# First batch's k and v loaded by halves of the heads, rms_g spread over the lanes by TensorE, the fifth tokens of q loaded behind the weights, and one turn of q issued behind the x turn

## The chip, the cores and the metric

The kernel runs on one core of one Trainium2 chip. The core has five engines that each work through their own instructions in order: TensorE (PE in the profile, with its weight loads as PEld), VectorE (DVE), ScalarE (ACT), GpSimd (POOL) and SyncE (SP), and 16 DMA engines that serve the queues of SP, ACT and POOL. Engines wait for each other by semaphores. The metric is the device time of one execution in microseconds; the time before is the median of three runs.

## The reference

The program is a linear attention with cosine weights, followed by a feed-forward block with an RMS norm and SwiGLU. With 8 batches, 8 heads, 576 tokens a batch and a head size of 64:

```python
r = np.maximum(x, 0.0); phi = np.concatenate([r * c, r * s], axis=-1)   # c, s: cos, sin of pi/2 * pos/S
kv = np.einsum('bhsf,bhsd->bhfd', k_p, v);  z = np.sum(k_p, axis=2)
num = np.einsum('bhsf,bhfd->bhsd', q_p, kv)
den = np.einsum('bhsf,bhf->bhs', q_p, z)[..., None] + 1e-06
x = (num / den).transpose(0, 2, 1, 3).reshape(B * S, H * D)             # 4608 x 512
xn = x / np.sqrt(np.mean(x * x, axis=-1, keepdims=True) + 1e-06) * rms_g
g = xn @ w_gate;  val = xn @ w_val                                      # 512 x 1536
out = (g / (1 + np.exp(-g)) * val) @ w_out                              # 1536 x 512
```

Inputs and output are float32.

## The kernel before

**Tiling.** A batch of 576 tokens is held in 128 lanes with four or five tokens a lane (`J = 4`, `NC5 = 5`); token slot `t` of all lanes is a tile of 128 tokens. Slots 0 to 3 of a batch make one block of 512 tokens; the fifth slots of two batches share a tile, and the four such tiles make a ninth block. The raw q, k and v lie in two buffers each (`qbuf`, `kbuf`, `vbuf`), so that batch `b` reuses the buffer of batch `b - 2`.

**A batch's attention.** `k_feat` makes the features of k: per slot two instructions, relu(k) times cosine and relu(k) times sine, on DVE or ACT (L246, L244). `v_cast` makes v bf16 (L258, L256). `kv_mm` (L291) multiplies them, 40 matmuls of 65 columns, and `kv_evict` copies the product to `kvm`: for batch 0 one half of the heads on ACT (L305) and the other on DVE (L307). `q_feat` makes the features of q, `q_turn` transposes them by a DMA of SP's queue (L316), or `q_turn_pe` does it on PE (L327) with `q_evict` after it (L336, L338). `num_mm` (L351) gives numerator and denominator, `divide` the quotient x (L377 to L389), `sumsq` the sum of squares on ACT (L400) and then its power of -1/2 on POOL (`rs`, L405), and `norm` multiplies x by `rs` and by `gb`, the gains rms_g in every lane (L410). The normed tile is transposed to `xnT` by `x_turn` (a DMA of SP's queue, L418) or `x_turn_pe` (L428) with `x_evict` (L435, L437).

**The feed-forward.** Nine blocks of twelve steps. A step makes 512 columns of gate and value products (L460 in pieces, L447 whole; tiles `gps`, `vps`), the silu on ACT (L685), the product on DVE (L695), and from block 2 on also the output products of the block before (L492). Block 0's output products are made in `lead()`, between blocks 0 and 1, with batch 1's attention in between.

**The order.** It is written out by hand. `at(g, w, f, ...)` puts work into place `w` of step `g` (12 steps to a block, counted through); the places run in the order sp, act0, dve0, mid, act1, act2, dve1, pe. `x_turn`s asked for under "sp" are issued right after dve0 of that step, work under "pe" after the step's matmuls. Each engine and each DMA queue works in this order; an instruction that waits holds up those behind it on its engine.

**The start.** SP issues the loads of batch 0: k, slots 0 and 1 of q, v, the gains broadcast to 128 lanes (`gb`, L138), slots 2 to 4 of q. Each load is two DMAs, one for the even and one for the odd lanes (L115). PE runs 44 matmuls on constants (`warm_up`), then the transposes of q. POOL makes constants, then `pool_after` (L238) copies one element of the first features of q, so that the weights, whose DMAs POOL issues next (L226, L232), come after them. From the ninth of POOL's DMAs on, each waits, by the built program, for the landing of the one eight before it. Batch 0's loads are all on SP's queue; from batch 1 to the k and v of batch 3 they are on POOL's, and later ones on SP's again.

Of the kernel before, what the change touches and what calls it, by code (L numbers as in the profile page):

```python
# [17 lines left out]
def kernel(  # L18
# [28 lines left out]
    def K(i):  # L47
        tc.keep_in_program_order(i)
        return i
# [27 lines left out]
    def gv_tile(shape, dtype, name):  # L77
        u = gv_out.pop(0)
        t = ps_gv.tile(shape, dtype, name=name, tag=f"gv{u}")
        gv_in[id(t)] = (u, t)  # L80
        return t

    def gv_read(t):

        if id(t) in gv_in:
            gv_out.append(gv_in.pop(id(t))[0])
# [20 lines left out]

    def load(t, src, b, odd_five=False, cuts=(0, NC5)):  # L110
        for lo, hi in zip(cuts[:-1], cuts[1:]):
            for par, t0, jn in lanes(odd_five):
                z = min(hi, jn)
                eng = nc.gpsimd if 0 < b < 3 or b == 3 and src is not q else nc.sync
                K(eng.dma_start(  # L115
                    out=t[par:P:2, :, lo * D : z * D],
                    in_=src[b, :, :, :].rearrange("h (i j) d -> i h (j d)", j=NT)[
                        :, :, (t0 + lo) * D : (t0 + z) * D
                    ],
                ))  # L120

    def load_v(b, cuts=(0, NC5)):
        load(vraw[b], v, b, False, cuts)

    def load_k(b):
        load(kraw[b], k, b)

    def load_q(b, cuts=(0, NC5)):
        load(qraw[b], q, b, b % 2 == 1, cuts)

    clear_fifth(kbuf[0], nc.vector)
    clear_fifth(qbuf[0], nc.vector)
    clear_fifth(vbuf[0], nc.vector)
    gb = consts.tile([P, DM], FP32, name="gb")
    load_k(0)
    load_q(0, (0, 2))
    load_v(0)
    K(nc.sync.dma_start(  # L138
        out=gb[:, :], in_=moe_rms_g.rearrange("(o d) -> o d", o=1).to_broadcast([P, DM])
    ))  # L140
    load_q(0, (2, NC5))


    iota_i = consts.tile([P, 1], mybir.dt.int32, name="iota_i")
# [41 lines left out]
    def table(c, u, j):  # L186
        n = u * J + j if j < J else 2 * J
        return trig[:, c, n : n + 1]
# [11 lines left out]
    vx = [consts.tile([P, H, E], BF16, name=f"vx{j}") for j in range(NC5)]  # L200
    kvm = [consts.tile([P, H, E], BF16, name=f"kvm{u}") for u in range(NK)]

    NX = 3
    xbuf = [consts.tile([P, DM + 1], FP32, name=f"x{u}") for u in range(NX)]
    for u in range(NX):
        nc.gpsimd.memset(xbuf[u][:, DM : DM + 1], math.sqrt(1e-6 * DM))
    warm = consts.tile([P, 2 * P], BF16, name="warm")
# [1 line left out]
    nc.vector.memset(warm[:, :], 1.0)  # L209
    for j in range(NC5):  # L210
        nc.gpsimd.memset(vx[j][:, :, D:E], 1.0)
    for t in (kbuf[1], qbuf[1], vbuf[1]):
        clear_fifth(t, nc.gpsimd)

# [9 lines left out]
    def load_gv(c):  # L224
        for (w, src) in ((wg, moe_w_gate), (wv, moe_w_val)):
            K(nc.gpsimd.dma_start(  # L226
                out=w[:, :, c * GC : (c + 1) * GC],
                in_=src[:, c * GC : (c + 1) * GC].rearrange("(t p) n -> p t n", p=P),
            ))
# [11 lines left out]
    def feat(dst, src, scale, act):  # L241

        if act:
            K(nc.scalar.activation(out=dst, in_=src, func=AF.Relu, scale=scale))  # L244
        else:
            K(nc.vector.tensor_scalar(  # L246
                out=dst, in0=src, scalar1=scale, scalar2=0.0, op0=ALU.mult, op1=ALU.max,
            ))

    def k_feat(b, j, c, act=False):  # L250
        feat(kp[j][:, :, c, :], kraw[b][:, :, j * D : (j + 1) * D], table(c, 0, j), act)

    def v_cast(b, j, act=False):
        src, dst = vraw[b][:, :, j * D : (j + 1) * D], vx[j][:, :, 0:D]
        if act:
            K(nc.scalar.copy(out=dst, in_=src))  # L256
        else:
            K(nc.vector.tensor_copy(out=dst, in_=src))  # L258
# [3 lines left out]
    def q_feat(b, t, c, act=False):  # L262
        if (b, t) not in qps:
            pool, tag = (qpp, "qp") if t < J else (qp5p, "qp5")
            qps[b, t] = pool.tile([P, H, 2, D], BF16, name=tag, tag=tag)
        feat(
            qps[b, t][:, :, c, :], qraw[b][:, :, t * D : (t + 1) * D], table(c, b % 2, t), act
        )

    def att_tile():  # L270

        return ring(ps_att, 2, [P, 2, TB], FP32, "att")

    def att_heads(a):
        return a[:, :, 0 : Z * E].rearrange("p z (s w) -> p z s w", w=E)

    def kv_banks(b):

        t = kvp[b]
        return t if b == 0 else [t[:, z, :] for z in range(2)]  # L280

    def kv_mm(b, j, first, last):
        if first:
            kvp[b] = (
                [gv_tile([P, TB], FP32, "kv0") for _ in range(2)]
                if b == 0 else att_tile()
            )
        banks = kv_banks(b)
        for h in range(H):

            K(nc.tensor.matmul(  # L291
                banks[h // Z][:, (h % Z) * E : (h % Z) * E + D + 1],
                lhsT=kp[j][:, h, :, :].rearrange("p c d -> p (c d)"),
                rhs=vx[j][:, h, 0 : D + 1],
                start=(first and h % Z == 0),
                stop=(last and h % Z == Z - 1),
            ))

    def kv_evict(b):
        dst = kvm[b % NK][:, :, :].rearrange("p (z s) w -> p z s w", z=2)  # L300
        if b == 0:
            for z, t in enumerate(kvp.pop(b)):
                src = t[:, 0 : Z * E].rearrange("p (s w) -> p s w", w=E)[:, :, 0 : D + 1]
                if z == 0:
                    K(nc.scalar.copy(out=dst[:, z, :, 0 : D + 1], in_=src))  # L305
                else:
                    K(nc.vector.tensor_copy(out=dst[:, z, :, 0 : D + 1], in_=src))  # L307
                gv_read(t)
        else:
            K(nc.scalar.copy(  # L310
                out=dst[:, :, :, 0 : D + 1], in_=att_heads(kvp.pop(b))[:, :, :, 0 : D + 1]
            ))

    def q_turn(b, t):
        tt = rqtp.tile([P, H, P], BF16, name="rqT", tag="rqT")
# [191 lines left out]
    def at(g, w, f, *a):  # L507
        plan[g, w].append(lambda: f(*a))
# [48 lines left out]
    at(3, "pe", x_turn_pe, (0, 3))  # L557
    at(4, "dve0", x_evict, (0, 3), 0, 3, True)
    for c in range(2):
        at(2 + c, "act2", q_feat, 0, J, c, True)  # L560


    at(0, "pe", load_wo, 2)
    at(0, "pe", load_k, 1)
    for f, *a in ((load_q, 1, (0, 2)), (load_v, 1), (load_q, 1, (2, NC5))):
        at(2, "pe", f, *a)
    for f in (load_k, load_q, load_v):
        at(3, "pe", f, 2)

    def pe_tile_at(g, key, xblk, col, gx, first="act1"):  # L570

# [29 lines left out]
        at(18, "act2" if j > 2 else "dve1", v_cast, 2, j, j > 2)  # L601
    kv_at(18, 2)
    pe_tile_at(19, (2, 0), 2, 0, 22, "act0")
    for t, g in enumerate((13, 19, 20, 21, 23)):
        q2_at(g, 2, t)
    pe_tile_at(22, (2, 1), 2, 1, 24)
    for t in (2, 3):
        tile_at(22 + t, (2, t), 2, t)


    at(15, "pe", load_q, 3)
    for j in range(NC5):
        for c in range(2):
            at(22 + j, "act2" if c else "dve1", k_feat, 3, j, c, c == 1)
# [152 lines left out]
            ))  # L767

    warm_up(44)
    for j in range(NC5):  # L770
        for c in range(2):
            if (j, c) in ((2, 1), (NC5 - 1, 1)):
                q_feat(0, 0, int(j > 2), act=(j > 2))
            k_feat(0, j, c, act=(j > 2))
    for c in range(2):
        q_feat(0, 1, c, act=(c == 1))
    pool_after(qps[0, 0][0:1, 0, 0, 0:1])
    for c in range(NG):
        load_gv(c)
    for c in range(2):  # L780
        load_wo(c)
    q_turn_pe(0, 0)
    q_evict(0, 0, dve=True)
    q_turn_pe(0, 1)
    q_evict(0, 1)
    warm_up(6)
    for j in range(NC5):
        v_cast(0, j, act=(j % 2 == 1))
    for j in (0, 1, 2, 4, 3):
        kv_mm(0, j, j == 0, j == 3)  # L790
    kv_evict(0)
    num_mm((0, 0))
    num_mm((0, 1))
    for c in range(2):
# [73 lines left out]
```

## Time and profile before

| | us |
|---|---|
| median of 3 runs (lowest to highest) | 332.92 (332.68 to 333.15) |
| the profiled execution's own time | 333.1 |
| its span, first to last instruction | 331.0 |
| busy: PE, DVE, ACT, POOL | 316.5, 189.5, 167.8, 42.7 |
| PE busy in the first 20 us | 13.50 |
| PE busy from 60 to 80 us | 18.25 |
| first gate product (L460) starts | 19.72 |

The profile lists, for each group of instructions, when they start, how long they take, and in square brackets how long the engine was idle before them and what ended the wait. A DMA's "us to landing" counts from the start of its issue until its data has arrived. About 2.1 us of the profiled time lie outside the span.

### The profile page before, as it was taken

The numbers are of one execution on the slowest core, as the hardware profiler recorded it, in microseconds if no ns is written. First come the engines' busy times: TensorE is split into PE (matmuls) and PEld (weight loads), VectorE is DVE, ScalarE is ACT, GpSimd is POOL, SyncE is SP. The second block draws the span as 40 slices with busy tenths as digits, with TensorE's granted clock in tenths as the row PEclk, the third lists the DMA queues.
The fourth block names the chain that finished last, engine by engine and source line by source line (L and its number), as shares of the span: only waits on it lengthen the run. The fifth ranks groups of instructions, "written<-read, shape, count | busy, mean of one in ns | idle before, by whom it ended". The sixth has DMA issues, their size and how long they took to land.

```text
span 331.0 us, 7153 instructions
## 1 busy us (share of the span) xinstructions
PE 316.5 (96%) x2805; PEld 210.5 (64%) x2840; DVE 189.5 (57%) x393; ACT 167.8 (51%) x318; POOL 42.7 (13%) x84
## 2 busy tenths in 40 slices
PE   6789999979999999999999999999999999999995
PEld 5579855979887777778777744554444444444443
DVE  4785386867966585687867676756543422222200
ACT  3765377757864366575646564644432322332221
POOL 3743344100101000011110001000100000000000
PEclk9999999999999999999999999999999999999999
DMA  7999999994268999997799898274124020000012
GB/s 217 303 206 207 291 336 384 373 199 84 47 128 224 305 235 314 228 296 154 175 225 289 165 239 135 67 94 111 50 63 111 34 63 32 35 32 32 34 63 95
DMA packets 80193, 55.26 MB, mean 167 GB/s; under 512 B 51200, under 2 KB 73488, under 8 KB 80160
## 3 DMA queue, kind: packets, MB, share of 16 engines
q1 hardware_dynamic: 72880, 40.52, 50.6%
q0 software_dynamic: 7120, 14.16, 16.5%
q8 instruction: 22, 0.36, 0.5%
q10 hardware_dynamic: 160, 0.13, 0.1%
q14 instruction: 11, 0.09, 0.1%
HBM read 38.01 MB, written 9.44 MB: 143 GB/s over the span
## 4 chain that ended last, share of the span: by engine, by line
PE 86%; DVE 4%; DMA 3%; issue 2%; ACT 2%; SPq 0%; POOL 0%; ACTq 0%; DVEq 0%
PE acc L492 25%; PE gps L460 15%; PE vps L460 14%; PE gps L447 12%; PE vps L447 12%; PE att L351 3%; PE att L291 3%; DMA kbuf<-in_k_dram 2%; DMA xnT<-xn 2%; DVE kp L246 1%; DVE xn L410 1%; PE acc L829 1%; PE qtp L327 1%; PE xps L428 1%; ACT kp L244 1%
## 5 line engine op out<-in xcount | busy, mean ns | idle before, releaser
L695 DVE TENSOR_TENSOR hT<-vps,sil 128x512 bf16<-128x512 f32 x108 | 74.6, 690 | 99.2 <-PE vps L447 58.3
L685 ACT ACTIVATE sil<-gps 128x512 bf16<-128x512 f32 x108 | 64.4, 596 | 100.0 <-PE gps L447 59.8
L492 PE MATMUL acc<-wo,hT 128*128 128x512 bf16 x396 | 101.8, 379 | 1.4 <-ACT osb L498 0.2
L492 PEld LDWEIGHTS <-hT 128*128 128x128 bf16 x420 | 40.5, 98 | 40.2 <-issue 0.4
L460 PE MATMUL gps<-xnT,wg 128*128 128x256 bf16 (+1 forms) x608 | 62.5, 250 | 2.5 <-DMA xnT<-xn 1.7
L460 PE MATMUL vps<-xnT,wv 128*128 128x256 bf16 (+1 forms) x608 | 62.5, 250 | 0.0
L460 PEld LDWEIGHTS <-wg 128*128 128x128 bf16 x608 | 48.0, 98 | 9.9 <-issue 2.5
L460 PEld LDWEIGHTS <-wv 128*128 128x128 bf16 x608 | 49.4, 98 | 4.2
L405 POOL TENSOR_TENSOR rs<-ss,mhalf 128x1 f32<-128x1 f32 x36 | 20.4, 567 | 199.1 <-ACT sq L400 199.1
L447 PE MATMUL gps<-xnT,wg 128*128 128x512 bf16 x139 | 36.7, 379 | 0.4
L447 PE MATMUL vps<-xnT,wv 128*128 128x512 bf16 x141 | 36.5, 379 | 0.1
L498 ACT COPY osb<-acc 128x512 f32<-128x512 f32 x35 | 20.5, 585 | 31.5 <-PE acc L492 27.7
L447 PEld LDWEIGHTS <-wv 128*128 128x128 bf16 x192 | 18.8, 98 | 22.7
L410 DVE SCALAR_TENSOR_TENSOR xn<-x,rs,gb 128x512 bf16<-128x512 f32 x36 | 26.9, 748 | 7.3 <-POOL rs L405 7.3
L447 PEld LDWEIGHTS <-wg 128*128 128x128 bf16 x192 | 18.0, 98 | 20.1
L400 ACT ACTIVATE sq<-x 128x513 f32<-128x513 f32 x36 | 22.6, 628 | 8.8 <-DVE x L389 8.5
L389 DVE TENSOR_TENSOR x<-att,rec 128x512 f32<-128x512 f32 x36 | 24.9, 691 | 1.2
L246 DVE TENSOR_SCALAR kp<-kbuf,trig 128x512 bf16<-128x512 f32 x50 | 22.7, 486 | 3.4 <-DMA kbuf<-in_k_dram 3.1
L246 DVE TENSOR_SCALAR qp<-qbuf,trig 128x512 bf16<-128x512 f32 x50 | 22.9, 479 | 0.0
L244 ACT ACTIVATE kp<-kbuf,trig 128x512 bf16<-128x512 f32 x30 | 20.7, 714 | 2.9 <-DMA kbuf<-in_k_dram 2.9
L244 ACT ACTIVATE qp<-qbuf,trig 128x512 bf16<-128x512 f32 x30 | 21.1, 712 | 0.2 <-DMA qbuf<-in_q_dram 0.2
L351 PEld LDWEIGHTS <-rqT 128*128 128x128 bf16 x320 | 14.4, 98 | 8.0 <-DVE rqT L336 0.9
(64 smaller groups left out, 183.3 us busy)
## 6 DMA issues: line engine op xcount, KB each, us to landing
out_dram<-osb SPq DMA_DIRECT2D x70, 128.0 KB, 2.1
kbuf<-in_k_dram SPq DMA_DIRECT2D x5, 640.0 KB, 5.6
vbuf<-in_v_dram SPq DMA_DIRECT2D x5, 640.0 KB, 6.7
qbuf<-in_q_dram SPq DMA_DIRECT2D x5, 640.0 KB, 6.8
kbuf<-in_k_dram SPq DMA_DIRECT2D x5, 512.0 KB, 4.5
vbuf<-in_v_dram SPq DMA_DIRECT2D x5, 512.0 KB, 6.0
qbuf<-in_q_dram SPq DMA_DIRECT2D x5, 512.0 KB, 5.0
kbuf<-in_k_dram POOLq DMA_DIRECT2D x3, 640.0 KB, 10.5
```

Source lines behind the costliest of these rows:

```text
L244: K(nc.scalar.activation(out=dst, in_=src, func=AF.Relu, scale=scale))
L246: K(nc.vector.tensor_scalar(out=dst, in0=src, scalar1=scale, scalar2=0.0, op0=ALU.mult, op1=ALU.max,))
L351: K(nc.tensor.matmul(nums[key][:, h // Z, (h % Z) * E : (h % Z) * E + D + 1], lhsT=rqT[a, t][:, h, :], rhs=kvm[a % NK][:, h, 0 : D + 1], s ...
L389: K(nc.vector.tensor_tensor(out=x[:, 0:DM].rearrange("p (z s d) -> p z s d", z=2, d=D), in0=a[:, :, :, 0:D], in1=r.unsqueeze(3).to_broadca ...
L400: K(nc.scalar.activation(out=sq[:, :], in_=xs[key][:, :], func=AF.Square, scale=1.0 / math.sqrt(DM), accum_out=ss[:, :],))
L410: K(nc.vector.scalar_tensor_tensor(out=xn[:, :], in0=xs.pop(key)[:, 0:DM], scalar=rss.pop(key)[:, :], in1=gb[:, :], op0=ALU.mult, op1=ALU. ...
L447: K(nc.tensor.matmul(ps[:, :], lhsT=w[:, dt, nn * P : (nn + 1) * P], rhs=xnT[blk][:, dt, :], start=(dt == 0), stop=(dt == NDT - 1),))
L460: K(nc.tensor.matmul(ps[:, i * cn : (i + 1) * cn], lhsT=w[:, dt, (n0 + i) * P : (n0 + i + 1) * P], rhs=xnT[blk][:, dt, c0 : c0 + cn], star ...
L492: K(nc.tensor.matmul(acc[blk][:, :], lhsT=hT[blk][:, nn, jt * P : (jt + 1) * P], rhs=wo[:, nn, :], start=(nn == 0), stop=(nn == NNT - 1),))
L498: K(nc.scalar.copy(out=osb[:, :], in_=acc[blk][:, :]))
L685: K(nc.scalar.activation(out=sil[:, :], in_=gp[:, :], func=AF.Silu))
L695: K(nc.vector.tensor_tensor(out=dst, in0=a, in1=c, op=ALU.mult))
```

## The change

- **k and v of batch 0 by halves of the heads.** `load` takes a slice of heads. k comes as four DMAs (heads 0 to 3, then 4 to 7), and so does v. `k_feat` and `v_cast` of batch 0 run per half: 20 feature instructions of 128x256 in place of 10 of 128x512, and 10 casts in place of 5. All of k's features now stand ahead of those of q, where two of q's stood between them. `kv_half` takes the place of `kv_mm` and `kv_evict` for batch 0: it multiplies one half of the heads for all slots and copies it out on DVE, then the other half.
- **rms_g spread by PE.** The broadcast DMA is gone. One DMA on ACT's queue brings the 512 gains to one lane. POOL splits them there into three bf16 parts (three copies and two subtractions of 1x512), and `spread_gains` adds the three parts up in all lanes by three matmuls against ones, copied to `gb` by ACT. In the built program POOL's order is: a copy, the mask of the identity matrix, a subtraction, a memset, a copy, a memset, a subtraction, a memset, a copy, and then `pool_after`; the three 128x512 memsets and the mask were there before.
- **q's fifth tokens.** Batch 0's SP load of q ends with slot 3; slot 4 (64 lanes, runs of 256 bytes) is a DMA of POOL's queue, behind the six of `wg` and `wv` and ahead of `wo`. Its features move from steps 2 and 3 to 8 and 9, and the load of batch 2's q, which reuses the buffer, from step 3 to step 9 and behind that of v.
- **One turn of q behind the x turn.** The features and the turn of slot 0 of batch 2's q move from step 13 to step 14, so that the turn is issued behind both `x_turn`s of batch 1 (steps 13 and 14). The load of batch 3's q moves from step 15 to 16.
- Six `warm_up` matmuls ahead of the first `kv_mm` are gone.

```diff
-    load_k(0)
+    g1, grest = xbuf[1][0:1, 0:DM], xbuf[2][0:1, 0:DM]
+    K(nc.scalar.dma_start(out=g1, in_=moe_rms_g.rearrange("(o d) -> o d", o=1)))
+    for hs in HALVES:
+        load(kraw[0], k, 0, hs=hs)
     load_q(0, (0, 2))
-    load_v(0)
-    K(nc.sync.dma_start(out=gb[:, :], in_=moe_rms_g.rearrange("(o d) -> o d", o=1).to_broadcast([P, DM])))
-    load_q(0, (2, NC5))
+    for hs in HALVES:
+        load(vraw[0], v, 0, hs=hs)
+    load_q(0, (2, J))
...
+    gpart = [kvm[NK - 1 - u][0:1, :, :].rearrange("p h e -> p (h e)")[:, 0:DM] for u in range(3)]
+    for u in range(3):
+        rest = g1 if u == 0 else grest
+        K(nc.gpsimd.tensor_copy(out=gpart[u], in_=rest))
+        if u < 2:
+            K(nc.gpsimd.tensor_tensor(out=grest, in0=rest, in1=gpart[u], op=ALU.subtract))
+    def spread_gains():
+        ps = gv_tile([P, DM], FP32, "gains")
+        for u in range(3):
+            K(nc.tensor.matmul(ps[:, :], lhsT=warm[0:1, 0:P], rhs=gpart[u], start=(u == 0), stop=(u == 2)))
+        K(nc.scalar.copy(out=gb[:, :], in_=ps[:, :]))
+        gv_read(ps)
...
-        at(2 + c, "act2", q_feat, 0, J, c, True)
+        at(8 + c, "act2", q_feat, 0, J, c, True)
...
-    for f in (load_k, load_q, load_v):
-        at(3, "pe", f, 2)
+    at(3, "pe", load_k, 2)
+    at(3, "pe", load_v, 2)
+    at(9, "pe", load_q, 2)
...
-    for t, g in enumerate((13, 19, 20, 21, 23)):
+    for t, g in enumerate((14, 19, 20, 21, 23)):
         q2_at(g, 2, t)
...
-    at(15, "pe", load_q, 3)
+    at(16, "pe", load_q, 3)
...
+    load_q(0, (J, NC5), eng=nc.gpsimd)
     for c in range(2):
         load_wo(c)
+    spread_gains()
     q_turn_pe(0, 0)
     q_evict(0, 0, dve=True)
     q_turn_pe(0, 1)
-    q_evict(0, 1)
-    warm_up(6)
-    for j in range(NC5):
-        v_cast(0, j, act=(j % 2 == 1))
-    for j in (0, 1, 2, 4, 3):
-        kv_mm(0, j, j == 0, j == 3)
-    kv_evict(0)
+    for z, hs in enumerate(HALVES):
+        for j in range(NC5):
+            v_cast(0, j, act=(j > 2), hs=hs)
+        if z == 0:
+            q_evict(0, 1)
+        kv_half(z, True)
```

## The prediction

> **What bounds the kernel now.** I read the page's busy shares first, then the windows of 20 us, then the timeline of the first 20 us and of 60 to 72 us, then the DMA landings and packets there.
>
> ```profile
> PE 316.5 (96%) x2805; PEld 210.5 (64%) x2840; DVE 189.5 (57%) x393; ACT 167.8 (51%) x318; POOL 42.7 (13%) x84
> ...
> 0.00:20.00 20.00, 13.50 (x158) 10.59 (x159) 13.01 (x40) 11.11 (x19) 10.44 (x31) 1.00 1.00 251
> 20.00:40.00 20.00, 19.77 (x258) 18.37 (x256) 11.04 (x20) 9.92 (x18) 7.38 (x11) 1.00 1.22 234
> 60.00:80.00 20.00, 18.25 (x288) 17.35 (x286) 13.84 (x30) 13.23 (x26) 1.66 (x3) 1.00 0.90 210
> ```
>
> PE (first figure after the length) is full from the first gate product on: 19.77 of 20 us. What PE has left to give lies in two places, the start and 1.75 us between 60 and 80. A delay of the start goes through to the end in full, since nothing behind it waits but PE.
>
> ```profile
> 2.67 0.52 POOL L99 MEMSET vbuf<- 128x512 f32 x1
> 2.75 0.46 DVE L158 CAST row_f<-row_i 128x4 f32<-128x4 int32 x1
> 7.24 2.07 DVE L246 TENSOR_SCALAR kp<-kbuf,trig 128x512 bf16<-128x512 f32 x5 [3.13 <-DMA kbuf<-in_k_dram]
> 9.77 0.37 POOL L238 COPY probe<-qp 1x1 bf16<-1x1 bf16 x1 [6.59 <-DVE qp L246]
> 10.08 0.92 POOL L226 DMA_DIRECT2D wg<-in_moe_w_gate_dram  x1
> 12.27 1.34 DVE L258 CAST vx<-vbuf 128x512 bf16<-128x512 f32 x3 [1.08 <-DMA vbuf<-in_v_dram]
> 14.52 0.43 DVE L307 CAST kvm<-kv 128x260 bf16<-128x260 f32 x1 [0.90 <-PE kv L291]
> 17.36 0.57 POOL L405 TENSOR_TENSOR rs<-ss,mhalf 128x1 f32<-128x1 f32 x1 [0.99 <-ACT sq L400]
> 19.72 1.05 PE L460 MATMUL gps<-xnT,wg 128*128 128x128 bf16 x16 [0.52 <-DVE xnT L435]
> ...
> 62.72 1.31 SPq L418 DMA_TRANSPOSE xnT<-xn  x1
> 64.22 1.24 SPq L316 DMA_TRANSPOSE rqT<-qp  x1
> 65.55 1.83 SPq L418 DMA_TRANSPOSE xnT<-xn  x1
> 71.14 1.03 PE L460 MATMUL gps<-xnT,wg 128*128 128x256 bf16 x8 [1.75 <-DMA xnT<-xn]
> ```
>
> In the start, data set the pace: DVE waits 3.13 us for k and 1.08 for v. From `kvm` (14.95) a fixed chain of numerator, quotient, `rs`, norm and turn leads to the gate product at 19.72. POOL and DVE meet once: a cast of four elements takes 0.46 us, and ends at 3.21, 0.03 behind the end of POOL's memset (3.19). They get in each other's way. At 71 PE waits for the second x turn, issued at 65.55 behind a turn of q.
>
> **The gap at 71.** The first x turn landed at 68.0 (62.72 + 5.3), q's turn at 70.5 (64.22 + 6.3), the second x turn at 71.0 (65.55 + 5.5). The norm that it needs was ready at 64.35 (0.74 from 63.61). With q's turn behind, SP issues it at 64.4, and it lands behind the first alone. q's turn, of twice the bytes, took 2.5 us after the first, so an x turn costs at most half: 69.3. PE stops at 71.14 - 1.75 = 69.39. I take 1.7 us off; ends 0 (it lands no sooner) and 1.75. q's turn is then late, landing about 70 to 72, but its numerator stands six steps on (75.9), and batch 3's q, which SP now issues behind it, is read ten steps on. The later load of batch 2's q lies in the stream of batch 2 (landed by 59.6) ahead of its first reader at step 14, near 64: nothing, and 0.5 us if that order turns late.
>
> **The start: loads.** Four halves of k cost SP two issues more (0.7 each), and so do v's. SP would issue v at 5.0, not 3.58, and q's slots 2 and 3 from 7.9, not 7.02; the data stay in line behind k and q until 8.9 and v until 12.2, which hides it; without that cover it is 1.4 us on v. The first half of k lands near 5.4, the second at 7.1 as before. `gb` leaves the queue: 12.9 - 12.2 = 0.7 us of DMA time, and q's fifth slot 0.3 more; that slot now lies ahead of `wo`, whose first reader is at 42.67 while the last `wo` lands at 38.5: hidden. Its features (0.71 each on ACT) at steps 8 and 9 lie in ACT's idle time. The six `warm_up`s ran in PE's idle time: nothing.
>
> **The start: POOL and DVE.** The gains land on one lane at about 2.7 (issue 0.74, and 2.0 to landing as for the last stores of ACT's queue). POOL's memsets, done by 3.19 before, now stand between its five new operations of 512 elements. The trace has no such operation. Nearest is the memset of 512, 0.52; the mask, 0.28 for 128 elements, gives 0.87 for a copy, and twice that for a subtraction with two inputs. So 2.6 to 6.0 us for five; I take 2.6 by the nearest row. With three memsets (0.46 apart), the mask and 0.4 of handovers that is 4.7 us: POOL would end at 7.4 alone. DVE has 12 half features before q's: five whole ones take 2.07, 0.40 apart; the 128x4 operations on constants run 0.13 apart, so a half is 0.27 (bounds 0.20, 0.40), 3.2 us in all, and 0.4 for q. If each waits for the other as at 3.2, the time adds up: from 5.4 on DVE owes 3.6 and POOL 2.0, plus 0.8 that DVE's operations on constants held POOL up; less 0.3 of POOL's handovers in which DVE works, q's first feature ends near 11.5, against 9.71. ACT, which shares nothing here, does eight half features of 0.45 and two of q by about 10.5.
>
> The Trainium skill's page "SBUF — State Buffer" (§ Who interferes with whom) says that a DVE cast or tensor_scalar in a two-port mode and a GpSimd instruction lock each other out for the whole instruction. The trace agrees where it can: 0.46 us for four elements. By a rule without the lock q's first feature would end at 9.4.
>
> The three matmuls (0.22 apart) and ACT's copy (0.59) lie in the wait for q's features.
>
> **The start: kv.** q's transpose and its eviction follow: 0.15 + 0.6 + 0.7 us, so DVE's casts of v begin near 12.9, not 12.27; its 1.08 us of idle time swallow the rest. Half the casts take 0.7, 20 matmuls 0.3 behind them, the eviction 0.43; then the same again, in line, where before both halves were evicted at once on two engines: `kvm` near 15.7, not 14.95. That is 0.8 us later, and so is 19.72. Without the lock it is 14.4, 0.5 earlier.
>
> **The start: a new wait.** With q's slot ahead, the second `wo` DMA is POOL's ninth and waits for the first `wg`; before, that was the third one, behind the first three `rs`. Now `rs` is queued behind it.
>
> ```profile
> wg<-in_moe_w_gate_dram POOLq DMA_DIRECT2D x1, 512.0 KB, 7.2
> ```
>
> `wg` landed at 17.3; then 0.8 to issue, `rs` at 18.1 instead of 17.36. After, the weights are issued at about 11.9 (11.5 + 0.37 as before), not 10.08. But POOL's queue (q0) got going only as SP's (q1) ran dry; the packets from 13 to 14 us, then from 14 to 15:
>
> ```profile
> q1 hardware_dynamic: 413, 0.31, 107.5%
> q0 software_dynamic: 6, 0.01, 3.6%
> ...
> q0 software_dynamic: 176, 0.18, 107.7%
> q1 hardware_dynamic: 69, 0.04, 15.2%
> ```
>
> SP's queue will be dry about 0.8 earlier, so `wg` lands between 16.5 and 19.1 (11.9 + 7.2). The sum of squares is ready at 17.3 + 0.8 = 18.1, so up to 17.3 this costs nothing; the late end costs 1.8. I take nothing, as the packets speak for the queue. Yet it takes the gain if there is no lock: `rs` cannot start before 17.3, as before. `wv`, which landed at 20.6 just as its first matmul began, lands 3.4 behind `wg`: 19.9 to 22.5 against a need at 21.5.
>
> **Sum.** 333.1 (the profiled execution; 0.2 above the median of 332.9) - 1.7 + 0.8 = 332.2; against the median 332.0. I say 332.1.
>
> **Rivals.** *No lock to speak of* (one lane's work releases it, or the gains come so late or so fast that they miss the features): the start stays at 19.7, held by `rs`, and the gap closes: 333.1 - 1.7 = 331.4, or 331.2 on the median. For it: `rs` on POOL does not slow features beside it. Against: 3.21.
>
> *POOL is slow, and the kernel slower:* if subtractions take 1.7 and copies 0.87, POOL holds DVE up by 3.4 us more, the start slips by 4.2, and the time is 335.6. It decides from 1.0 us more than I took (a slip of 1.8), where the gap's gain is used up. At subtractions of 1.1 the slip is 2.0: 333.4. For it: two inputs, and float32 in; against: the memset's row.
>
> The skill's page "GPSIMD Engine Reference" (§ Elementwise — side-by-side cycle accounting) gives 2.6 cycles an element for two inputs. At its 1.2 GHz that is an estimate of 1.1 us a subtraction; no run here shows it yet.
>
> *The gap does not close:* the second x turn is held by k and v of batch 3, which land until 67.6, and not by q's turn: half to none of 1.7 comes back, 333.0 to 333.9. Against it: it landed 0.5 behind q's turn.
>
> **How the numbers follow.** The forecast (slip 0.2 to 1.4, gap closed; 331.5 to 332.7) has 0.38, no lock 0.27, POOL slow 0.22 (half of it above 333.6), the gap open 0.13. A change of 0.2% (0.67 us) is about what a measurement here can tell from none. Faster: no lock and most of the forecast, 0.55; within 0.2%: the rest of the forecast and the lower half of slow POOL, 0.20; slower: 0.25. The range takes in no lock and the start 0.2 better, 331.0, and slow POOL up to a slip of 2.9, 334.2.
>
> **What would show it.** PE's wait for `xnT` near 70 gone. POOL's copies and subtractions at 0.5 us; k's half features on DVE drawn out to 0.4 or more on average where POOL works; q's first feature near 11.5, `kvm` near 15.7, the first gate product near 20.5. It is wrong if the features run 0.27 apart beside POOL, if a subtraction takes over 1 us, or if `rs` waits for `wo`.

## The result and the profile after

The changed kernel takes 334.05 us (median of 22 runs, 332.69 to 334.99) against 332.94 for the kernel before (22 runs): ratio 1.003, 95% interval 1.0019 to 1.0041. It is slower by 0.3%, where a gain was forecast; the time lies within the range.

The profiled execution of the changed kernel took 332.95 us (span 331.1), level with the one of before (333.1, span 331.0). It is not typical: its mean granted clock (the share of TensorE's full clock that it was given) is 1.000, which 2 of the 22 runs had (332.69 and 332.95); the other 20 had 0.987 to 0.995 and 333.13 to 334.99. So its trace shows the change at the full clock; what the other runs lose needs a trace of its own, below.

The page's shares, of the changed kernel:

```profile
PE 317.1 (96%) x2802; PEld 210.5 (64%) x2837; DVE 194.1 (59%) x403; ACT 168.8 (51%) x324; POOL 47.4 (14%) x90
```

Its windows of 20 us (length, then busy time of PE, PEld, DVE, ACT and POOL with counts, granted clock, DMA share, GB/s):

```profile
0.00:20.00 20.00, 13.42 (x145) 10.11 (x145) 16.52 (x46) 11.61 (x25) 14.53 (x37) 1.00 0.96 231
20.00:40.00 20.00, 19.03 (x253) 17.67 (x252) 11.76 (x23) 9.20 (x18) 7.98 (x12) 1.00 1.22 234
...
60.00:80.00 20.00, 19.55 (x310) 18.64 (x308) 15.17 (x33) 14.05 (x28) 1.66 (x3) 1.00 0.90 225
```

PE loses 0.74 between 20 and 40 us (19.77 before) and wins 1.30 between 60 and 80 (18.25 before): the start is later, and the gap at 71 smaller. The timeline of the changed kernel (start, duration, engine, line, operation) has both:

```profile
2.75 1.33 DVE L167 CAST row_f<-row_i 128x4 f32<-128x4 int32 x1
2.91 1.14 POOL L226 TENSOR_TENSOR x<-x,kvm 1x512 f32<-1x512 f32 x1
5.21 1.52 DVE L189 TENSOR_SCALAR th<-th 128x9 f32<-128x9 f32 x1
5.56 1.14 POOL L226 TENSOR_TENSOR x<-x,kvm 1x512 f32<-1x512 f32 x1
7.02 3.59 DVE L271 TENSOR_SCALAR kp<-kbuf,trig 128x256 bf16<-128x256 f32 x12 [0.29 <-ACT trig L193]
10.54 0.86 DVE L271 TENSOR_SCALAR qp<-qbuf,trig 128x512 bf16<-128x512 f32 x2
12.40 1.00 DVE L283 CAST vx<-vbuf 128x256 bf16<-128x256 f32 x3
13.97 0.43 DVE L337 CAST kvm<-kv 128x260 bf16<-128x260 f32 x1 [0.57 <-PE kv L303]
14.31 1.11 DVE L283 CAST vx<-vbuf 128x256 bf16<-128x256 f32 x3
14.53 0.79 POOL L251 DMA_DIRECT2D wg<-in_moe_w_gate_dram  x1
15.26 0.80 POOL L251 DMA_DIRECT2D wv<-in_moe_w_val_dram  x1
15.93 0.43 DVE L337 CAST kvm<-kv 128x260 bf16<-128x260 f32 x1 [0.51 <-PE kv L303]
17.68 0.74 POOL L257 DMA_DIRECT2D wo<-in_moe_w_out_dram  x1 [0.17 <-issue]
18.77 0.57 POOL L433 TENSOR_TENSOR rs<-ss,mhalf 128x1 f32<-128x1 f32 x1 [0.35 <-ACT sq L428]
21.20 1.00 PE L488 MATMUL gps<-xnT,wg 128*128 128x128 bf16 x15 [0.52 <-DVE xnT L463]
...
63.95 2.78 SPq L446 DMA_TRANSPOSE xnT<-xn  x2
66.91 1.42 SPq L344 DMA_TRANSPOSE rqT<-qp  x1
71.07 1.03 PE L488 MATMUL gps<-xnT,wg 128*128 128x256 bf16 x8 [0.45 <-DMA xnT<-xn]
```

POOL's subtractions on the gains last 1.14 us, and each holds a small operation of DVE until it ends (2.75 + 1.33 = 4.08, 2.91 + 1.14 = 4.05; 5.21 + 1.52 = 6.73, 5.56 + 1.14 = 6.70). So the cosine table comes late and k's features start at 7.02; from there they run 0.27 apart but for one (0.62, beside POOL's last copy). q's first feature ends at 11.01. The casts of v start at 12.40, 0.13 later than before; `kvm` is complete at 16.36, 1.41 later (14.95), and the first gate product starts at 21.20, 1.48 later (19.72). At 71 PE waits 0.45 instead of 1.75 us and goes on at 71.07 instead of 71.14: at the full clock the smaller gap gives back what the start lost.

### The profile page after: what moved, and what is told of

It is laid out like the page before. It is cut to its first block, busy times and chain, and to the rows that moved or that the text cites. A ratio compares the mean times of both kernels' runs of the same rounds, so it can differ in the third digit from the quotient of the medians.

```text
span 331.1 us, 7177 instructions
## 1 busy us (share of the span) xinstructions
PE 317.1 (96%) x2802; PEld 210.5 (64%) x2837; DVE 194.1 (59%) x403; ACT 168.8 (51%) x324; POOL 47.4 (14%) x90
## 4 chain that ended last, share of the span: by engine, by line
PE 86%; DVE 7%; issue 2%; DMA 2%; ACT 1%; POOL 0%; ACTq 0%; DVEq 0%
PE acc L520 26%; PE gps L488 14%; PE vps L488 14%; PE gps L475 12%; PE vps L475 12%; PE att L379 3%; PE att L303 3%; DMA xnT<-xn 2%; DVE kp L271 2%; DVE xn L438 1%; PE qtp L355 1%; PE xps L456 1%; DVE x L417 1%; DMA out_dram<-osb 1%; DVE vx L283 1%
## 5 line engine op out<-in xcount | busy, mean ns | idle before, releaser
L433 POOL TENSOR_TENSOR rs<-ss,mhalf 128x1 f32<-128x1 f32 x36 | 20.4, 567 | 197.0 <-ACT sq L428 197.0
L271 DVE TENSOR_SCALAR kp<-kbuf,trig 128x512 bf16<-128x512 f32 (+1 forms) x56 | 23.5, 457 | 0.6 <-PE att L303 0.3
L269 ACT ACTIVATE kp<-kbuf,trig 128x512 bf16<-128x512 f32 (+1 forms) x34 | 21.4, 663 | 0.0
```

The source lines that it names most:

```text
L271: K(nc.vector.tensor_scalar(out=dst, in0=src, scalar1=scale, scalar2=0.0, op0=ALU.mult, op1=ALU.max,))
```

## The experiments

The theory that the runs led to, called the clock theory below: most runs are slow because PE is busy too little between 9 and 20 us, so that the granted clock falls, and the slip of the start is a second loss, which the turn gives back. Its rivals: the slip alone makes the time, and differs from run to run with the landing of the gains; and the gains on POOL, not the halves, make the slip. Times are medians; ratios are to the kernel before, run beside them.

**The changed kernel once more, unedited.**

> The changed kernel itself once more, for a second trace. Theory A (its times spread because the one-lane gains land at different times, and every later POOL operation then holds up DVE): where the time is above 333.5, the first POOL cast of the gains starts later than the 2.08 us of the first trace, and the first gate product starts later than 21.20 by about as much. Rival B (the spread comes from DMA traffic behind the start): the first gate product starts at 21.2 +- 0.2 whatever the time, and PE's idle time between 20 and 100 us differs.

It took 334.20 us (9 runs), ratio 1.0042 (1.003 to 1.0053); one run had clock 1.000 and took 332.98, all others 333.99 or more. Now the profiled one was a common one (333.99, clock 0.987). Its windows of 1 us, same columns as above, and its first gate product:

```profile
10.00:11.00 1.00, 0.26 (x2) 0.00 (x0) 1.00 (x5) 1.00 (x3) 0.00 (x0) 1.00 1.08 367
11.00:12.00 1.00, 0.67 (x12) 0.69 (x13) 0.60 (x3) 1.00 (x3) 0.75 (x2) 1.00 1.13 329
12.00:13.00 1.00, 0.47 (x10) 0.30 (x7) 1.00 (x3) 1.00 (x4) 1.00 (x2) 1.00 1.05 258
13.00:14.00 1.00, 0.80 (x15) 0.70 (x16) 0.57 (x2) 1.00 (x3) 1.00 (x3) 0.59 0.57 56
14.00:15.00 1.00, 0.47 (x9) 0.30 (x6) 0.49 (x2) 1.00 (x4) 1.00 (x3) 0.50 0.93 130
...
19.00:20.00 1.00, 1.00 (x11) 0.93 (x10) 0.77 (x3) 0.61 (x3) 0.34 (x1) 0.50 1.27 215
```

```profile
22.31 1.05 PE L488 MATMUL gps<-xnT,wg 128*128 128x128 bf16 x16 [0.52 <-DVE xnT L463]
```

The third figure from the right is the granted clock: 0.50 from 13.2 to 20.0. The chain to the first gate product crosses PE several times (sums of kv, numerator, transposes), and it ends at 22.31, 1.11 after the full-clock run; the whole time differs by 333.99 - 332.95 = 1.04. The gains landed at nearly the same time in both (POOL's first cast starts at 2.24 and 2.08). By the first cast of v (12.59 and 12.40) this run was 0.18 late, which leaves some 0.93 of the 1.11 to the clock: the landing of the gains does not make the difference.

The clock's record in the traces says more. In every trace the stretch between two changes of the clock is a whole multiple of 3.41 us long (here 6.83 at half, from 13.19 to 20.01), and the changes lie at different moments in different executions. In all seven falls that were traced ahead of the kernel's end, PE had been busy for 0.37 to 0.57 of the 3.41 us before (here 0.53, from 9.77 to 13.19). In the first trace the three such stretches between 10.46 and 20.70 had 0.62, 0.61 and 0.60, and the clock stayed. So, as far as the traces show, the same program keeps or loses its clock by how the 3.41 us happen to lie over its sparse stretch. The line is not sharp: of some 1480 stretches at the full clock that no fall followed, three were as low (0.44, 0.55, 0.57).

**The reordered turn alone** (the kernel before with two lines of the change).

```diff
-    for t, g in enumerate((13, 19, 20, 21, 23)):
+    for t, g in enumerate((14, 19, 20, 21, 23)):
-    at(15, "pe", load_q, 3)
+    at(16, "pe", load_q, 3)
```

> The kernel before with the turn of q behind the x turn alone (and batch 3's q one step later). Theory: the wait of 1.75 us near 71 goes, the rest stays: 331.2 to 331.6, ratio 0.995 to 0.996. Rival (the second x turn is held by batch 3's k and v, which land until 67.6): the wait stays above 1 us, 332.2 or more.

332.09 us (9 runs, 331.67 to 332.22), ratio 0.9974 (0.9964 to 0.9984): faster than both kernels, and the best of this study. Its timeline:

```profile
62.85 2.78 SPq L418 DMA_TRANSPOSE xnT<-xn  x2
65.81 1.49 SPq L316 DMA_TRANSPOSE rqT<-qp  x1
...
70.09 1.03 PE L460 MATMUL gps<-xnT,wg 128*128 128x256 bf16 x8 [0.58 <-DMA xnT<-xn]
```

The wait falls from 1.75 to 0.58, not to nothing: the two x turns land at 69.33 and 69.96. The second is 0.63 behind the first, but the first itself lands 1.3 later than before (68.0), while k and v of batch 3 come in until 67.6.

**The change without the reordered turn** (13 and 15 again).

> The changed kernel with q's turn ahead of the second x turn again, as before. Theory (the reorder is what closed the gap): PE waits 1.3 to 1.8 us near 71 and the time is 1.0 to 1.4 above the changed kernel's in the same rounds. Rival (the gap closed because PE came 1.5 us later while the DMA stream did not): PE waits 0.3 to 0.6 us, and the time is the changed kernel's within 0.3.

335.36 us (4 runs), ratio 1.0076 (1.0048 to 1.0104). The profiled one, at clock 0.995:

```profile
67.10 1.56 SPq L446 DMA_TRANSPOSE xnT<-xn  x1
...
72.28 1.03 PE L488 MATMUL gps<-xnT,wg 128*128 128x256 bf16 x8 [1.38 <-DMA xnT<-xn]
```

The turn is worth some 1.2 us in the changed kernel too; everything else in the change costs about 2.6 (335.36 against 332.78 of the kernel before in the same rounds).

**The change with the gains by a broadcast DMA** behind v, as in the kernel before; no operations on POOL, no matmuls.

```diff
-    K(nc.scalar.dma_start(out=g1, in_=moe_rms_g.rearrange("(o d) -> o d", o=1)))
...
+    K(nc.sync.dma_start(
+        out=gb[:, :], in_=moe_rms_g.rearrange("(o d) -> o d", o=1).to_broadcast([P, DM])
+    ))
...
-    spread_gains()
```

> The changed kernel with the gains broadcast by SP's DMA behind v again, in place of POOL's split and PE's spread. Theory A (POOL's five operations and DVE lock each other out, and that is the whole slip): cosine table ready near 4.4 instead of 6.99, kvm near 14.4 to 14.9, first gate product at 19.5 to 19.9, time 331.2 to 331.7, and the spread of the runs as small as before (0.5 us). Rival (the halves or the wait of rs behind the second wo DMA hold the start): first gate product above 20.3, time above 332.

333.44 us (10 runs), ratio 1.0024 (1.0012 to 1.0036). Nothing blocks DVE early now, and q's first feature ends at 10.16. Yet `kvm` is complete at 16.41, as late as with the gains on POOL:

```profile
15.98 0.43 DVE L322 CAST kvm<-kv 128x260 bf16<-128x260 f32 x1 [0.69 <-PE kv L288]
```

The clock was 0.50 from 14.9 to 18.4 (mean 0.988 to 0.995 in all ten), which slowed the second half's sums: the wait before this eviction is 0.69 instead of 0.51, some 0.2 of the slip. So the fall of the clock does not come from the gains, nor does most of the slip; what the halves alone make of it at the full clock stands below.

**The kernel before with the gains on POOL**, and nothing else.

```diff
-    K(nc.sync.dma_start(
-        out=gb[:, :], in_=moe_rms_g.rearrange("(o d) -> o d", o=1).to_broadcast([P, DM])
-    ))
+    for u in range(3):
+        rest = g1 if u == 0 else grest
+        K(nc.gpsimd.tensor_copy(out=gpart[u], in_=rest))
+        if u < 2:
+            K(nc.gpsimd.tensor_tensor(out=grest, in0=rest, in1=gpart[u], op=ALU.subtract))
...
+    spread_gains()
```

> Kernel before with the gains split on POOL and spread by PE instead of the broadcast DMA, and nothing else. Prediction's step on the lock: subtractions 1.14 us, casts 0.6 (as measured with all parts), q's first feature ends 10.4 to 11.0 instead of 9.71. If that goes through: casts of v from about 12.5 to 12.8, first gate product 19.9 to 20.3, time 333.0 to 333.5. If the wait for v (12.18) swallows it: first gate product within 0.15 of 19.72, time 332.7 to 333.0. If the 0.7 us of DMA time that gb leaves free matters: v lands by 11.9.

332.91 us (10 runs), ratio 1.0006 (0.9991 to 1.0021): no difference. From its timeline:

```profile
9.57 0.48 DVE L261 TENSOR_SCALAR qp<-qbuf,trig 128x512 bf16<-128x512 f32 x1
...
12.30 1.28 DVE L273 CAST vx<-vbuf 128x512 bf16<-128x512 f32 x3
...
20.01 1.05 PE L475 MATMUL gps<-xnT,wg 128*128 128x128 bf16 x16 [0.52 <-DVE xnT L450]
```

q's first feature ends at 10.05 instead of 9.71; the casts still wait for v, and the gate product moves by 0.29.

**The kernel before with k and v by halves**, the six `warm_up`s ahead of each half, `gb`, q's slots and the turns as before.

```diff
-    load_k(0)
+    for hs in HALVES:
+        load(kraw[0], k, 0, hs=hs)
...
-    q_evict(0, 1)
-    warm_up(6)
-    for j in range(NC5):
-        v_cast(0, j, act=(j % 2 == 1))
-    for j in (0, 1, 2, 4, 3):
-        kv_mm(0, j, j == 0, j == 3)
-    kv_evict(0)
+    for z, hs in enumerate(HALVES):
+        warm_up(6)
+        for j in range(NC5):
+            v_cast(0, j, act=(j > 2), hs=hs)
+        if z == 0:
+            q_evict(0, 1)
+        kv_half(z, True)
```

> Kernel before with k and v of the first batch by halves of the heads (loads, features, casts, sums), six warm_up matmuls ahead of each half's casts, and gb, q's fifth tokens and the turns as before. If the halves make most of the slip at the full clock: kvm lands 15.9 to 16.5, not 14.95, first gate product 20.8 to 21.4, not 19.72, and the time is 333.8 to 334.6 (before plus 1.0 to 1.7). If the slip comes from POOL's operations on the gains: kvm by 15.2, time within 0.4 of before.

333.67 us (10 runs), ratio 1.0028 (1.0006 to 1.005). Its timeline:

```profile
11.63 1.38 DVE L268 CAST vx<-vbuf 128x256 bf16<-128x256 f32 x3
...
13.86 1.37 DVE L268 CAST vx<-vbuf 128x256 bf16<-128x256 f32 x3
...
15.74 0.43 DVE L322 CAST kvm<-kv 128x260 bf16<-128x260 f32 x1 [0.51 <-PE kv L288]
...
20.95 1.27 PE L473 MATMUL gps<-xnT,wg 128*128 128x128 bf16 x16 [0.52 <-DVE xnT L448]
```

The halves alone move `kvm` by 1.22 and the gate product by 1.23. The first half's casts start 0.64 earlier than the whole casts did, so the part from the first cast of v to `kvm` takes 4.54 us instead of 2.68 (3.96 in the changed kernel). Three half casts should take 0.7 and take 1.4. The clock was full up to the gate product here (it fell at 21.6), so this slip is not the clock's.

**The changed kernel with the weights held back**, which takes away what POOL does beside the second half's casts.

```diff
     pool_after(qps[0, 0][0:1, 0, 0, 0:1])
-    for c in range(NG):
-        load_gv(c)
-    load_q(0, (J, NC5), eng=nc.gpsimd)
-    for c in range(2):
-        load_wo(c)
+    load_gv(0)
     spread_gains()
...
         kv_half(z, True)
+    pool_after(kvm[0][0:1, H - 1, 0:1])
+    load_gv(1)
...
     sumsq((0, 1))
+    for c in range(2, NG):
+        load_gv(c)
+    load_q(0, (J, NC5), eng=nc.gpsimd)
+    for c in range(2):
+        load_wo(c)
```

> Changed kernel, with POOL's weight DMAs behind the first pair issued later: the second pair behind the first batch's kvm, the third pair, q's fifth tokens and wo behind the two rs. In the traces so far every half cast of v on DVE that starts beside a POOL weight DMA's issue (0.77 us each, one behind the other) ends 0.116 behind the end of that issue (0.60 to 0.63 instead of 0.27). Theory that DVE's casts and POOL's DMA issues take turns: the second half's three casts take 0.27 each, kvm lands near 15.9 instead of 16.36, rs starts right behind its sum, first gate product 20.6 to 20.8 instead of 21.2. Rival (the half casts are slow by themselves, or by the DMA traffic): second half's casts still 0.6, kvm 16.3 or later, first gate product 21.1 or later. Median 333.2 to 334.0 by the first, for the clock stays as it is; above 334.2 if the held weights are late for their first matmul.

334.34 us (4 runs), ratio 1.0042 (1.0027 to 1.0057). The timeline, then the window of 1 us in which the eviction ends:

```profile
14.31 0.69 DVE L283 CAST vx<-vbuf 128x256 bf16<-128x256 f32 x3
...
15.72 0.43 DVE L337 CAST kvm<-kv 128x260 bf16<-128x260 f32 x1 [0.72 <-PE kv L303]
```

```profile
16.00:17.00 1.00, 0.80 (x13) 0.76 (x13) 0.49 (x3) 0.24 (x1) 0.43 (x2) 0.50 1.24 202
```

The three casts take 0.69 instead of 1.11, 0.284 to 0.286 each. So a DMA issue of POOL (0.77 us each, one behind the other) blocks a cast that begins beside it. The changed kernel's rows agree: the casts that ended at 13.21, 14.69 and 15.43 began 0.28 to 0.52 us into an issue, and these issues ended at 13.09, 14.57 and 15.31, 0.12 earlier each; the three of 0.27 to 0.28 us began within 0.1 us of an issue's start. `kvm` came only 0.2 earlier, since the sums behind the casts ran at half the clock. The same with PE kept busy:

**Weights held back, and 25 matmuls of `warm_up` added** (q's slot and `wo` issued in the first step).

```diff
+        warm_up(6)
         for j in range(NC5):
             v_cast(0, j, act=(j > 2), hs=hs)
...
     q_turn_pe(0, 2)
-    warm_up(5)
+    warm_up(14)
...
     x_turn_pe((0, 0))
+    warm_up(4)
```

> Changed kernel with the weight DMAs behind the first pair issued later (second pair behind kvm, third behind the second rs, q's fifth tokens and wo in the first step) and with the added warm_up matmuls of the run before. If the casts blocked by POOL's DMA issues make a large part of the late start: second half's casts 0.28 each, kvm 15.6 to 15.85 (16.36 in the changed kernel), first gate product 20.4 to 20.7 (21.2), median 332.5 to 332.9. If they do not, and the halves are late because the two halves' casts and evictions stand in one line on DVE: kvm 16.1 or later, first gate product 21.0 or later, median 333.2 to 333.4 as with the warm_ups alone.

333.11 us (10 runs), ratio 0.9998 (0.9979 to 1.0017), and nine of ten runs at clock 0.997 or more. Its timeline:

```profile
14.35 0.43 DVE L337 CAST kvm<-kv 128x260 bf16<-128x260 f32 x1 [0.56 <-PE kv L303]
14.69 0.69 DVE L283 CAST vx<-vbuf 128x256 bf16<-128x256 f32 x3
15.94 0.43 DVE L337 CAST kvm<-kv 128x260 bf16<-128x260 f32 x1 [0.56 <-PE kv L303]
...
21.21 1.00 PE L488 MATMUL gps<-xnT,wg 128*128 128x128 bf16 x15
```

From the first half's eviction to the second's it is 1.59 us instead of 1.96: the blocked casts cost 0.37 there. In this run q's first feature ended at 11.39, 0.38 later than in the changed kernel (the gains landed later: POOL's first cast starts at 2.41, not 2.08), and so the gate product did not move. `kvm`, at 16.37, lies beyond the bound set for blocked casts that matter little (16.1), but without the later start it would be near 15.99, between the two bounds. So the second half's blocked casts make 0.37 of the 1.41 by which `kvm` is late. That most of the rest is the second half's casts, sums and eviction standing in line on DVE behind the first half's fits the rows (1.59 for the second half alone, with no cast blocked), but no run tests it by itself.

**The clock: matmuls added to the changed kernel.** First six `warm_up`s ahead of each half's casts, twelve in all:

```diff
     for z, hs in enumerate(HALVES):
+        warm_up(6)
```

> Changed kernel with six warm_up matmuls put ahead of each half's casts of v (twelve in all, the kernel before had six). Clock theory (PE is busy too little between 9 and 16 us, so the granted clock is halved for some us in nearly every run): the granted clock is 1.00 in every us from 9 to 22, the mean clock 0.998 or more in nearly all runs, first gate product near 21.2, median 332.7 to 333.2 and a spread of under 0.6 us. Start theory (the slip of the start alone makes the time, the clock is only its shadow): the median stays at 333.8 to 334.4. If the warm_ups themselves stand in the way of the transposes: first gate product above 21.6.

333.60 us (10 runs), ratio 1.0021 (1.0002 to 1.004); clock 1.00 in every us from 9 to 22 of the profiled run (332.93), whose first gate product starts at 21.33. Six of ten runs have 0.997 or more, five of them at 332.86 to 333.27 and one at 333.92; the four with 0.994 or 0.995 take 334.02 to 334.95. Then also the 13 further down (14 for 5, and 4), as in the diff of the run before:

> Changed kernel with six warm_up matmuls ahead of each half's casts of v (as in the run with twelve), and with the second warm_up(5) behind q's third transpose made 14 and four more behind the first x transpose, so that PE has work in its idle time from 18.6 to 21.2 too. Clock theory: mean clock 0.997 or more in at least 8 of 10 runs, median 332.8 to 333.1, nearly no run above 333.5, and the changed kernel is then level with the kernel before. Rival (runs near 334 have another cause than the clock): clock 0.997 or more, yet times spread to 334 as with twelve. If the added matmuls stand in the way of the chain: first gate product above 21.5.

333.30 us (10 runs), ratio 1.0016 (1.0006 to 1.0027); nine of ten at 0.998 or more. So the share of runs at 0.997 or more goes from 3 in 31 (the changed kernel, both times) to 6 in 10 and 9 in 10, and the median from 334.05 to 333.6 and 333.3. The traces show why twelve were not enough: of the 3.41 us that start at 9 us or later, the sparsest had PE busy 0.45 of the time in the changed kernel's first trace (from 17.8) and still 0.45 with the twelve (from 17.9), which stand ahead of it, but 0.74 with all 25; in the kernel before it is 0.55. The clock theory holds for more than half of the excess (1.11 us over the kernel before, 0.46 with the 25). Not for all of it: two runs at clock 0.998 and 0.999 took 335.02 and 334.66. The first of them is the profiled one:

```profile
142.79 3.40 SPq L446 DMA_TRANSPOSE xnT<-xn  x1
...
147.57 2.52 SPq L344 DMA_TRANSPOSE rqT<-qp  x1
...
155.72 1.05 PE L488 MATMUL gps<-xnT,wg 128*128 128x256 bf16 x8 [1.91 <-DMA xnT<-xn]
```

Two turns issued behind loads of k and v held SP for 3.40 and 2.52 us, where the changed kernel has 1.20 and 1.25, and PE waits 1.91 us for an x turn at 154, where it did not. Whether the other outliers are of this kind wasn't traced.

**The kernel before without its six `warm_up`s.**

```diff
-    warm_up(6)
     for j in range(NC5):
         v_cast(0, j, act=(j % 2 == 1))
```

> Kernel before without its six warm_up matmuls ahead of the casts of v, and nothing else. Clock theory: the granted clock falls to about 0.5 for 2 to 5 us between 12 and 18 us in most runs, and the time is 0.4 to 1.2 above before: 333.2 to 334.1. Rival (kv of the kernel before is dense enough without them, only the halves make PE too idle): within 0.2 of before, clock 0.998 or more.

332.89 us (10 runs), ratio 0.9994 (0.9981 to 1.0007): no difference, though four of ten runs fell to 0.994 or 0.995 (of 92 runs of the kernel before beside the experiments, four had 0.995 or less). Those four took 332.63 to 333.37. So without the six the clock falls more often in the kernel before, but the median does not show it. With the halves, which stretch the sums, it falls in 28 of 31 runs without `warm_up`s there, and in three of ten (the halves alone) and four of ten (the whole change) with twelve. The halves with just the six were not run.

**q's fifth tokens behind the weights, alone** (with q of batch 2 loaded from step 9).

```diff
-    load_q(0, (2, NC5))
+    load_q(0, (2, J))
...
     for c in range(NG):
         load_gv(c)
+    load_q(0, (J, NC5), eng=nc.gpsimd)
```

> Kernel before with q's fifth tokens of the first batch loaded behind the weights by POOL (and q of batch 2 loaded from step 9), and nothing else. If the second wo DMA, now ahead of rs on POOL, matters: it is issued when the first wg lands (17.2), rs starts at 17.9 to 18.1 instead of 17.36, first gate product 20.2 to 20.5, time 333.0 to 333.6. If it is hidden: first gate product within 0.2 of 19.72 and time 332.6 to 332.9. If the DMA time freed ahead of v or before the x turns matters: PE's wait at 71 under 1.5 us, time below 332.5.

334.18 us (10 runs, 332.74 to 336.09), ratio 1.0028 (1.0004 to 1.0053). Its timeline:

```profile
17.05 0.19 ACT L403 ACTIVATION_READ_ACCUMULATOR sq<-x 128x1 f32 x1
17.32 0.74 POOL L235 DMA_DIRECT2D wo<-in_moe_w_out_dram  x1 [1.11 <-DMA wg<-in_moe_w_gate_dram]
...
18.08 1.11 POOL L408 TENSOR_TENSOR rs<-ss,mhalf 128x1 f32<-128x1 f32 x2
...
20.43 0.80 PE L463 MATMUL gps<-xnT,wg 128*128 128x128 bf16 x6 [0.52 <-DVE xnT L438]
```

The sum of squares is ready at 17.24; the second `wo` DMA, released by `wg`, takes POOL until 18.07, and `rs` starts 0.72 later than before. The gate product is 0.71 later, and PE, waiting meanwhile, drops to a clock of 0.50 from 19.9 to 23.4 us in this run. Five of the ten runs had 0.995 and took 334.57 to 336.09, the other five 332.74 to 333.8.

**v of batch 3 later, beside the reordered turn**, to take away the loads under which the x turns land.

```diff
-        load_v(3)
+    at(14, "pe", load_v, 3)
```

> Kernel before with q's turn one step later and q's load two steps later (as the turn alone was run), and v of batch 3 loaded from step 14 on instead of ahead of the stream. If transfers of k and v of batch 3, that land until 67.6, hold what is left of PE's wait at 70 (0.58): the second x turn lands before 69.4, no wait there, 331.3 to 331.7. If not: 331.9 to 332.3 as with the turn alone; if v is then late for its own readers: above 332.4.

335.65 us (4 runs), ratio 1.0074 (1.0047 to 1.0101). Its timeline, and the window behind the wait:

```profile
63.63 1.50 POOL L115 DMA_DIRECT2D vbuf<-in_v_dram  x2
...
72.12 1.03 PE L460 MATMUL gps<-xnT,wg 128*128 128x256 bf16 x8 [2.56 <-DMA xnT<-xn]
```

```profile
74.00:75.00 1.00, 1.00 (x15) 0.88 (x14) 0.36 (x1) 0.81 (x2) 0.00 (x0) 0.50 1.08 365
```

POOL, with nothing else to do, issued v at 63.6, right between the x turns, and PE's 2.56 us without work were followed by a clock of 0.50 to 0.69 in the four windows from 73 to 77. Step 17 instead of 14:

> Kernel before with q's turn one step later and q's load two steps later (the turn alone), and v of batch 3 loaded from step 17 instead of ahead of the stream (step 14 put it into the x turns' way: PE's wait was 2.6 us). If the transfers of k and v, and not the order of the turns, hold the second x turn now: it lands before 69.4, PE's wait near 70 is gone, 331.3 to 331.7. If k alone or something else holds it: 331.9 to 332.2. If v is then in the way of q's later turns or of its readers: above 332.4.

335.53 us (10 runs, 333.70 to 337.24), ratio 1.007 (1.0049 to 1.0091). v was issued at 63.52 again: a place in the plan orders a DMA against POOL's own work, and POOL had none after 63.6. Still, both runs show that these loads hold the turns: with v issued behind it, the first x turn landed at 67.50 and 67.30, not 69.33, and the second, now behind v, 0.56 and 0.57 after v had landed (71.42 and 71.49). What is left of the wait could not be closed this way.

## Why the prediction was wrong, step by step

**The step that failed most** is "The six `warm_up`s ran in PE's idle time: nothing". They ran in idle time, but took part in what set the granted clock. Without them, and with the sums of kv drawn out from 12.7 to 15.9, 28 of 31 runs had a mean granted clock of 0.987 to 0.995; in the one of them that was traced it was half the clock for 6.8 us on the very chain that sets the start, and cost some 0.93 us. With twelve matmuls put in, the median goes from 334.05 to 333.6, with 25 to 333.3. How much of the loss six would have saved is open. The Trainium skill's page "TensorE: Matmul & The Clock Gate" (Part 1) says that PE's clock falls to half after about one idle window of 3.4 us, and that this window runs freely, so that its phase differs between runs. The traces agree in the two values 1.00 and 0.50, in the steps of 3.41 us, and in that these lie differently from run to run. They differ in what is enough: none of the seven stretches before a fall was idle, PE was busy for 0.37 to 0.57 of them (in the run shown 0.26, 0.67 and 0.47 of the us from 10 to 13, before the fall at 13.2).

**The sizes.** Without the clock's loss the changed kernel would still not have been faster, but level (with matmuls put back, the runs at 0.997 or more lie between 332.65 and 333.5 but for a few). Two terms of the sum were mis-sized.

- *kv*, +0.8 predicted: +1.41 measured. The casts began at 12.40, earlier than the 12.9 of the sum, and then "the same again, in line" took 3.96 us, not 2.86. Casts at 0.7 a half took 1.00 and 1.11, blocked by DMA issues, and 0.3 from the last cast to the eviction was 0.57 and 0.51.
- *the gap*, -1.7 predicted: the wait fell by 1.17 with the turn alone (-0.69 us between the medians). That q's turn lay between the two was right, and the second x turn does land close behind the first there (0.63). But the first was taken to land as before, and it lands 1.3 later. That k and v of batch 3 hold it, as that rival had it, is borne out in part: with v issued behind it, it landed 1.8 to 2.0 earlier. But v then held the second turn, so that the gap without these loads was not seen. In the changed kernel the wait falls by 1.30; its second x turn lands at 70.94, 1.85 behind the first, and PE, which is 1.2 later itself, waits less for it.

**POOL and DVE.** The lock was right, its place and size were not. A subtraction took 1.14 us, not 0.52 (the Trainium skill's page "GPSIMD Engine Reference", § Elementwise — side-by-side cycle accounting, gave the estimate 1.1; measured 1.14). It did not draw out k's features, but held the cosine table before them: `trig` is ready at 6.99, not 4.36. q's first feature came at 11.0 instead of 11.5, and alone the whole is worth 0.29 at the gate product and nothing in the time: the casts wait for v either way. The rival of a slow POOL, with 2.0 of slip at 1.1 a subtraction, is refuted by that run. So is the rival without the lock: with the gains by DMA it took 333.44, not 331.2, for the halves and the clock stay.

**The loads.** The splits were not free: the second half of k landed at 7.86 (7.1 before) and v at 12.99 (12.2), where "the data stay in line" was assumed. The casts of the second half began at 14.31, which hid it.

**The new wait.** `rs` behind the second `wo` DMA, taken at nothing, costs 0.72 when q's slot is moved alone. In the changed kernel it does not show, because everything before `rs` is late by more: that DMA's issue ends at 18.42, the sum of squares is ready at 18.69, and `rs` starts 0.08 behind it, as in the kernel before (17.28 and 17.36). The prediction gave the right bound (0 to 1.8) and said what would reveal it; it should have counted it with a `kvm` on time. It also means that repairing the halves alone would not bring the gate product before about 20.9 here, by an estimate: `wg` at 17.39, 1.04 from there to `rs` as in that run, and 2.43 from `rs` to the gate product as in the changed kernel.

**What was right.** PE carries the time and a late start goes through; the wait at 71 nearly goes; `wg` landed at 17.39 (16.5 to 19.1) and `wv` at 20.65 (19.9 to 22.5); no wait of PE for batch 2's q shows.

## What to carry to other kernels

Matmuls on constants in a sparse stretch are not idle weight: before they are dropped, or the stretch is lengthened, read the granted clock by the microsecond in several runs, since one profile at the full clock can be the exception. Splitting work into halves that stand in line on one engine adds each half's fixed waits, and each short piece meets the other engine's instructions anew. Parts of a change that all delay the same chain do not add up (1.23, 0.71 and 0.29 alone, 1.48 together), so each is to be priced with the others on time, and the one that gains, here two lines of order, is worth taking by itself.

## What the runs showed that was not expected

- A DMA issue on POOL of 0.77 us blocks a DVE cast from SBUF to SBUF. In all the traces of half casts (128x256), those that started 0.25 to 0.52 us into an issue ended 0.11 to 0.12 us past the issue's end (0.37 to 0.64 us instead of 0.27 to 0.29); those that started within 0.15 us of the issue's start ran through. The Trainium skill's page "SBUF — State Buffer" (§ Who interferes with whom) tells of the other direction, a DMA of POOL's queue starved by DVE, and says that whoever issues first blocks the other; the traces agree, with the DMA's issue as the first, from 0.25 us into it on.
- A stall of PE can cost more than its length: 2.56 us without work at 70 were followed by four windows of 1 us at 0.50 to 0.69 of the clock, with PE full.
- What a fall of the clock costs depends on where it lies. At half from 15.2 to 18.6, in the change without the reordered turn, the first gate product came 0.29 later (21.49, with the casts of v at 12.41 as in the first trace). With q's fifth tokens moved alone, where the trace has it from 19.9 to 23.4 and PE is full from 20.4 on, the low runs took 334.57 us and more, the others 333.8 and less. And in the kernel before without its `warm_up`s two of the four low runs took 332.63 and 332.67, no more than the others.
- The issue of a turn on SP can take 3.40 instead of 1.20 us behind loads of k and v, which in one execution cost PE 1.91 us at 154, far from the change.
